# A weight's last rows on few partitions: 32 partitions in two steps instead of 20 in three, read as eight groups of four rows instead of five

## The chip, the cores and the metric

The kernel runs on one core of one Trainium2 chip. The metric is the device time of one execution, in microseconds (us), as the median of several runs; lower is better. The profile comes from one further execution that was recorded instruction by instruction and packet by packet.

## The reference, cut to what matters

One decoding step for a batch of two sequences: a layer norm, grouped-query attention over a cache of 4096 positions (16 query heads, 8 key and value heads, head size 256), and a bilinear gated unit whose result gates the attention's output.

```python
x = A_x                                     # (2, 1, 448)
xn = _layernorm(x, axis=-1)
s = _A_ref(xn, A_k_cache, A_v_cache, A_wq, A_wo)
g = _silu(_B_ref(xn, B_w_gate, B_w_up, B_w_down))
return x + s * g

# _A_ref
q = (x @ wq).reshape(B, Sq, Hq, Dh).transpose(0, 2, 1, 3)
k = jnp.repeat(k_cache, rep, axis=1)        # 2 query heads share a key head
v = jnp.repeat(v_cache, rep, axis=1)
p = softmax(einsum("bhqd,bhkd->bhqk", q, k) * Dh ** -0.5)
return (einsum("bhqk,bhkd->bhqd", p, v) ...).reshape(B, Sq, Hq * Dh) @ wo

# _B_ref
return ((x @ w_gate) * (x @ w_up)) @ w_down
```

All arrays are float32. The two caches hold 67 MB each; wq (448 x 4096), wo (4096 x 448) and the three matrices of the gated unit (448 x 1792, twice, and 1792 x 448) make up the rest of the 158.6 MB that are read.

## The kernel before

**Loads.** The 16 pairs of a key head and a batch row are worked off one after another; pair i needs `k{i}` (4 MB) and `v{i}` (4 MB). All loads go through one queue, that of the sync engine (SP), in an order fixed by `plan` (lines 85 to 96): `wq0`, `wqx`, `k0`, then the fused loads `vk` (value block i and key block i + 1 in one load of 8 MB), between them the weights (`wgu` after the first, `wdq` after the third, `wo` after the ninth), at the end `k15` and `v14`, and `v15` with the last eight blocks of `wo` in seven pieces. `issue` (line 65) sends the next ones: three at the start, then one or two after the scores of each pair. The tiles of the ring have two buffers and the weights share one slot, so that a load waits until the buffer's last reader is done. The 16 DMA engines each take a share of the rows of a load, one after another in the order of the queue.

**The query projection.** `query(0)` makes the queries of the first four key heads from `wq0` and `wqx`, `query(1)` (after pair 4) those of the others from `wq1`, which comes with `wdq`. A weight with 448 rows is folded onto 128 partitions (`folded`, line 444): rows 0 to 383 are three full steps of 128 rows for each of four column tiles (12 blocks of 512 columns), and the last 64 rows of the four tiles, two tiles to a block, are blocks 12 and 13. `rows` (line 191) multiplies: 12 matmuls with the full steps (line 199), then the rest by `last` (line 200), where `xf` holds the normalized input's last 64 values twice, on partitions 0 to 63 and 64 to 127, with zeros beside them, so that one matmul serves two column tiles.

**wqx.** For `wq0` alone, block 12 (the last 64 rows of tiles 0 and 1) isn't loaded on 128 partitions. It comes as `wqx`, on 20 partitions (`SIDE`): three steps (`NS`) of 20 rows for each of the two tiles, and four rows (`LEFT`) of both tiles together on eight partitions; seven pieces of 512 columns in all (`EXTRA`). In main memory it is stored as five groups of four rows with a fifth, empty row behind each (line 456), and the load takes `wqx[:, :4]`. So `wq0` has 13 blocks of 512 columns on 128 partitions. The matmuls are those of lines 206 to 212: six with 20 rows against `xeT`, `last(1, 12)` for block 13 among them, and one with eight rows against `xl`. `xeT` and `xl` are made at the start: transposes at lines 155 and 156, copies at 157 and 161, and two selects on GpSimd (lines 162 to 165) that zero the half of `xl` that belongs to the other tile. Because block 12's second half begins with the four rows that share a piece, `folded` rolls these rows by `LEFT`, and lines 129 and 130 write the normalized input's tail in the same rolled order.

**The rest.** Per pair: scores (line 265), softmax, transposition, values (line 309); the results are collected in `ob` and projected with `wo`. At the end the values of pair 15 (line 409) run as the pieces of `v15` land, and the last blocks of `wo` (lines 413 to 420) as theirs land. `manual_schedule` keeps the order of the code on each engine.

Of the kernel before, what the change touches and what calls it, by code (L numbers as in the profile page):

```python
# [10 lines left out]
OP = mybir.AluOpType  # L11
AX = mybir.AxisListType

B, D = 2, 448
HKV, REP, SK, DH = 8, 2, 4096, 256
F = 1792
NT = 4
W = 32
DUP = W // 2
NK = 4  # L20
# [6 lines left out]
LATE = 24  # L27
THIRD = [24, 25, 26, 28, 29, 30, 31, 27]
PART = 14 * (D + 512)
SIDE = 20  # L30
NS = 3
EXTRA = 2 * NS + 1
LEFT = 64 - NS * SIDE
EPS = 1e-5


# [5 lines left out]
def gated_decode_block(ctx: ExitStack, tc: tile.TileContext, x, first, vk, last0, last1, wq0, wqx, wdq, wo, wgu, out):  # L42
    nc = tc.nc
# [11 lines left out]
    def bank(name=None):  # L55
        return psum.tile([128, 512], F32, name=name, bufs=1) if name else two()[:, 0]
# [8 lines left out]
    def issue(n=1):  # L65
        for names, src, cuts in todo[:n]:
# [12 lines left out]
            if names == ["wq0"]:  # L79
                at = src.shape[1]  # L80
                loaded["wqx"] = t[:, at:at + EXTRA * 512]
                nc.sync.dma_start(loaded["wqx"][:SIDE], wqx[:, :4])
        del todo[:n]
# [23 lines left out]
    ident = const.tile([128, 128], F32)  # L107
# [6 lines left out]
    xc = e0[:, 1, :D]  # L114
# [8 lines left out]
    rstd = const.tile([B, 1], F32)  # L123
# [2 lines left out]

    xn = e1[:, 1]
    nc.vector.tensor_scalar(xn[:, :D], xc, rstd, None, op0=OP.mult)  # L128
    nc.vector.tensor_scalar(xn[:, D:D + LEFT], xc[:, D - LEFT:], rstd, None, op0=OP.mult)
    nc.vector.tensor_scalar(xn[:, D + LEFT:], xc[:, 384:D - LEFT], rstd, None, op0=OP.mult)  # L130
    pt = bank()
    for k in range(NK):
        nc.tensor.transpose(pt[:, B * k:B * (k + 1)], xn[:, k * 128:(k + 1) * 128], ident[:B, :B])  # L133
    def copies(dst, pt):
        n, b = pt.shape
        nc.vector.tensor_copy(dst.rearrange("p k (b j) -> p k b j", b=B),
                              pt.rearrange("p (k b) -> p k b", b=B)[:, :, :, None].to_broadcast([n, b // B, B, DUP]))
# [5 lines left out]
    spare = oT1.rearrange("p g d r m -> p (g d r) m")  # L143

    xf = spare[:, NK:NK + 2]
# [4 lines left out]

    xeT = spare[:SIDE, :NS]
    pt = bank()
    for j in range(NS):
        at = 384 + j * SIDE
        nc.tensor.transpose(pt[:SIDE, B * j:B * (j + 1)], xn[:, at:at + SIDE], ident[:B, :B])
    nc.tensor.transpose(pt[:2 * LEFT, B * NS:B * (NS + 1)], xn[:, D - LEFT:D + LEFT], ident[:B, :B])
    copies(xeT, pt[:SIDE, :NS * B])

    xl = spare[:2 * LEFT, NK + 2:NK + 4]
    for a in range(2):  # L160
        copies(xl[:, a:a + 1], pt[:2 * LEFT, NS * B:(NS + 1) * B])
    nc.gpsimd.affine_select(out=xl, in_=xl, compare_op=OP.is_ge, fill=0.0, base=0, pattern=[[-LEFT, 2], [0, W]],
                            channel_multiplier=1)
    nc.gpsimd.affine_select(out=xl, in_=xl, compare_op=OP.is_ge, fill=0.0, base=LEFT - 1, pattern=[[LEFT, 2], [0, W]],
                            channel_multiplier=-1)

    both = work.tile([128, D], F32, name="h")[:B, :W].rearrange("p (b j) -> p b j", b=B)
    nc.vector.tensor_copy(both, ident[:B, :B, None].to_broadcast([B, B, DUP]))
    pt = bank()
    for c in range(NT):  # L170
        nc.tensor.matmul(pt[W * c:W * (c + 1), :SL], both.rearrange("p b j -> p (b j)"), x2[:, c * SL:(c + 1) * SL],
                         start=True, stop=True)
# [18 lines left out]
    def rows(ps, w, n, extra=None):  # L191


        def block(i):
            return w[:, i * n:(i + 1) * n]

        for k in range(3):
            for c in range(NT):
                nc.tensor.matmul(ps[W * c:W * (c + 1), :n], xnT[:, k, :], block(NT * k + c), start=k == 0, stop=False)  # L199
        def last(a, i):  # L200
            nc.tensor.matmul(ps[64 * a:64 * (a + 1), :n], xf.rearrange("p a j -> p (a j)"), block(i), start=False, stop=True)  # L201

        if extra is not None:

            for j in range(NS):
                for c in range(2):
                    at = (c * NS + j) * n
                    nc.tensor.matmul(ps[W * c:W * (c + 1), :n], xeT[:, j, :], extra[:SIDE, at:at + n], start=False, stop=False)  # L208
                if j == 0:
                    last(1, 12)  # L210
            nc.tensor.matmul(ps[:2 * W, :n], xl.rearrange("p a j -> p (a j)"), extra[:2 * LEFT, 2 * NS * n:(2 * NS + 1) * n],  # L211
                             start=False, stop=True)
            return
        for a in range(2):
            last(a, 12 + a)


    qT = [const.tile([128, B, 4, 2, REP, DUP], F32, name=f"qT{h}") for h in range(2)]
# [1 line left out]
    def query(h):  # L220
        ps = bank()
        rows(ps, loaded[f"wq{h}"], 512, None if h else loaded["wqx"])
        for r in range(REP):
            nc.vector.transpose(qT[h][:, :, :, :, r, :].rearrange("p b g d j -> p (g d) b j"),
                                ps[:, r * 256:(r + 1) * 256])
# [16 lines left out]
    def ffn_in():  # L242
        pp = two()
        for i, w in enumerate(("wg", "wu")):
            rows(pp[:, i], loaded[w], FC)
        g = work.tile([128, FC], F32, name="h")
        nc.scalar.copy(g, pp[:, 0, :FC])
        h = work.tile([128, FC], F32, name="h")
        nc.vector.tensor_mul(h, pp[:, 1, :FC], g)
        nc.vector.transpose(hT.rearrange("p i m -> p (i m)"), h)  # L250
# [34 lines left out]
    def softmax(i, s, m, pT=None):  # L285
        sm = bank("sm")
        nc.tensor.transpose(sm[:1, :128], m[:, 0:1], ident)  # L287
        mx = work.tile([1, NT, W], F32, name="mx", bufs=1)
        nc.vector.tensor_reduce(  # L289
            mx, sm[:1, None, :128].rearrange("p o (c j) -> p o j c", c=NT).to_broadcast([1, NT, W, NT]),  # L290
            axis=AX.X, op=OP.max)
        nc.tensor.transpose(sm[:, 128:129], mx.rearrange("p c j -> p (c j)"), one)  # L292
        nc.vector.tensor_scalar(m[:, 1:2], sm[:, 128:129], -1.0 / 16, None, op0=OP.mult)  # L293
        p = work.tile([128, 2, 512], F32, name="p", bufs=1)
        nc.scalar.activation(p, s, AF.Exp, bias=m[:, 1:2], scale=1.0 / 16, accum_out=su[:, place(i):place(i) + 1])  # L295
        if pT is None:
            pT = work.tile([128, 2, 512], F32, name="pT", bufs=1)
        nc.vector.transpose(pT.rearrange("p h n -> p (h n)"), p.rearrange("p h n -> p (h n)"))  # L298
        return pT
# [65 lines left out]
    p = softmax(0, *ss)  # L365
    for i in range(LAST):
# [10 lines left out]
        p = softmax(i + 1, *ss)  # L377
# [19 lines left out]
    ps = [p]  # L397
    project(oT1, 4, EARLY, LATE)

    last = slot.tile([128, PART], F32, name="slot", align_bytes=512)  # L400
    p = softmax(LAST + 1, *ss, last[:, :1024].rearrange("p (h n) -> p h n", h=2))
# [78 lines left out]
```

## Time and profile before

| | |
|---|---|
| median of 3 runs | 376.34 us (376.27 to 376.48) |
| span of the profiled execution | 374.6 us |
| bytes read | 158.56 MB |
| mean granted TensorE clock | 0.775 |

The profiled execution's own time is its span, from the first instruction to the last, and what lies around it. On the page, the 40 digits of a row are the busy share of 40 equal slices of the span, in tenths; the DMA row is a mean over 16 DMA engines. A row of instructions or loads gives the line, the engine, the operation, the tile written and the tiles read, and the number of instructions. In a row of a table by windows stand the window, its length, the busy time of TensorE's matmuls and weight loads, VectorE, ScalarE and GpSimd with the number of instructions of each, the granted clock, the share of the DMA engines' time and GB/s. q1 is SP's queue of loads, q8 and q14 are instruction fetches, q10 is the load of x.

### The profile page before, as it was taken

The page shows a single profiled execution, that of the slowest core. Times are in us where ns is not written, and L with a number is a line of the kernel's source. Part 1 is how long each engine was busy: PE and PEld are TensorE (multiplying, and loading weights), DVE is VectorE, ACT ScalarE, POOL GpSimd, SP SyncE. Part 2 cuts the span into 40 slices and gives each one's busy share as a digit, 9 for nine tenths or more (in the row PEclk, how much of TensorE's full clock was granted, in tenths as well). Part 3 has the DMA queues.
Part 4 walks back from the last instruction along what each step waited for, and adds up shares of the span by engine and source line. Part 5 has one row for each costly group of instructions (what it writes and reads, how often), then busy time and mean ns, then how long its engine had stood idle before and what let it go on. Part 6 is the DMA issues. An engine that isn't in the chain of part 4 may idle for free.

```text
span 374.6 us, 3092 instructions
## 1 busy us (share of the span) xinstructions
PE 197.4 (53%) x1388; PEld 55.3 (15%) x1388; DVE 72.6 (19%) x125; ACT 25.8 (7%) x40; POOL 1.7 (0%) x9
## 2 busy tenths in 40 slices
PE   0793459081726090858271756712718180909785
PEld 0210112020201020212020211200202020202122
DVE  2303030104040003040404050400211212030530
ACT  1001010001020002010101010100010101010121
POOL 0000000000000000000000000000000000000000
PEclk9968596778696587796778696885868586777999
DMA  8999899999999999999999999999999999999994
GB/s 327 435 493 434 376 438 441 448 443 437 431 428 443 441 434 420 422 427 434 436 448 448 427 426 397 452 448 448 436 427 420 436 427 420 448 411 441 411 416 186
DMA packets 4217, 158.81 MB, mean 424 GB/s; under 512 B 599, under 2 KB 857, under 8 KB 1241
## 3 DMA queue, kind: packets, MB, share of 16 engines
q1 hardware_dynamic: 4201, 158.62, 98.2%
q8 instruction: 11, 0.18, 0.2%
q10 hardware_dynamic: 4, 0.00, 0.0%
q14 instruction: 1, 0.01, 0.0%
HBM read 158.56 MB, written 0.06 MB: 423 GB/s over the span
## 4 chain that ended last, share of the span: by engine, by line
DMA 74%; PE 23%; issue 1%; DVE 1%; ACT 0%; POOL 0%; ACTq 0%; SPq 0%; DVEq 0%
DMA ring<-vk 67%; PE o L313 10%; PE s L274 8%; DMA ring<-last 5%; DMA p<-x 2%; PE s L199 1%; PE s L208 1%; PE s L313 1%; PE s L211 1%; PE s L356 0%; PE s L201 0%; PE wide L351 0%; ACT ob L410 0%; PE cb L322 0%; DVE pT L121 0%
## 5 line engine op out<-in xcount | busy, mean ns | idle before, releaser
L313 PE MATMUL o<-ring,pT 128*32 128x512 f32 x480 | 83.2, 856 | 115.6 <-DMA ring<-vk 115.6
L275 DVE TENSOR_REDUCE m<-s 128x1 f32<-128x1024 f32 x16 | 19.6, 1222 | 219.9 <-PE s L274 219.9
L274 PE MATMUL s<-ring,qT 128*32 128x512 f32 x512 | 59.6, 607 | 0.9 <-PE s L211 0.9
L313 PEld LDWEIGHTS o<-ring,pT 128*32 128x32 f32 x480 | 20.8, 150 | 168.6 <-issue 156.1
L295 ACT ACTIVATE p<-s,m 128x1024 f32<-128x1024 f32 x16 | 17.8, 1113 | 286.1 <-DVE m L293 286.1
L274 PEld LDWEIGHTS s<-ring,qT 128*32 128x32 f32 x512 | 17.2, 112 | 40.7 <-issue 38.1
L298 DVE STREAM_TRANSPOSE pT<-p 128x1024 f32<-128x1024 f32 x15 | 18.7, 1245 | 21.2 <-ACT p L295 21.2
L199 PE MATMUL s<-slot,xnT 128*32 128x512 f32 (+1 forms) x96 | 15.3, 788 | 3.3 <-DMA slot<-wgu 3.3
L287 PE MATMUL sm<-ident,m 128*1 128x128 f32 x16 | 4.3, 270 | 18.8 <-DVE m L275 18.8
L289 DVE TENSOR_REDUCE mx<-sm 1x128 f32<-1x512 f32 x16 | 10.7, 671 | 2.9 <-PE sm L287 2.9
L292 PE MATMUL sm<-one,mx 1*128 1x1 f32 x16 | 3.6, 226 | 14.2 <-DVE mx L289 14.2
L373 DVE COPY ob<-o 128x512 f32<-128x512 f32 x14 | 9.5, 681 | 0.0
L256 PE MATMUL s<-slot,hT 128*32 128x448 f32 x28 | 5.8, 918 | 4.4 <-DMA slot<-wdq 4.4
L351 PE MATMUL wide<-slot,oT 128*32 128x448 f32 x48 | 6.4, 684 | 0.7 <-DVE oT L340 0.6
L287 PEld LDWEIGHTS sm<-ident,m 128*1 128x1 f32 x16 | 1.3, 79 | 32.9 <-DVE m L275 32.3
L133 PE MATMUL s<-ident,pT 2*128 2x2 f32 x4 | 0.6, 246 | 10.4 <-DVE pT L128 10.4
L322 PE MATMUL cb<-ob,add_blocks 128*32 128x512 f32 (+2 forms) x48 | 4.1, 456 | 2.4 <-DVE ob L373 1.6
L199 PEld LDWEIGHTS s<-slot,xnT 128*32 128x32 f32 x96 | 3.5, 137 | 11.7 <-issue 11.7
L292 PEld LDWEIGHTS sm<-one,mx 1*128 1x128 f32 x16 | 2.3, 142 | 17.2 <-DVE mx L289 17.2
L295 ACT ACT_TABLE_LOAD x2 | 2.6, 1283 | 30.6 <-DVE m L293 23.5
L313 PE MATMUL s<-ring,slot 128*32 128x512 f32 x32 | 4.2, 600 | 0.8 <-DMA ring<-last 0.8
L201 PE MATMUL s<-slot,oT 128*64 128x448 f32 (+1 forms) x14 | 4.6, 664 | 0.0
(76 smaller groups left out, 47.5 us busy)
## 6 DMA issues: line engine op xcount, KB each, us to landing
ring<-last SPq DMA_DIRECT2D x2, 4096.0 KB, 24.8
slot<-wdq SPq DMA_DIRECT2D x1, 6720.0 KB, 45.5
slot<-wgu SPq DMA_DIRECT2D x1, 6272.0 KB, 32.7
slot<-wo SPq DMA_DIRECT2D x1, 5376.0 KB
ring<-first SPq DMA_DIRECT2D x1, 4096.0 KB, 20.6
slot<-wq SPq DMA_DIRECT2D x1, 3328.0 KB, 10.7
ring<-last SPq DMA_DIRECT2D x1, 2048.0 KB
ring<-last SPq DMA_DIRECT2D x1, 1536.0 KB, 17.8
```

The costliest lines, as they stand in the source:

```text
L199: nc.tensor.matmul(ps[W * c:W * (c + 1), :n], xnT[:, k, :], block(NT * k + c), start=k == 0, stop=False)
L256: nc.tensor.matmul(ps[W * t:W * (t + 1), :D], hT[:, i], loaded["wd"][:, i * D:(i + 1) * D], start=i < NT, stop=i >= 14 - NT)
L274: nc.tensor.matmul(s[W * c:W * (c + 1), h, :], q[:, d], k[:, h, d, c, :], start=d == 0, stop=d == 1)
L275: nc.vector.tensor_reduce(m[:, 0:1], s, axis=AX.XY, op=OP.max)
L287: nc.tensor.transpose(sm[:1, :128], m[:, 0:1], ident)
L289: nc.vector.tensor_reduce(mx, sm[:1, None, :128].rearrange("p o (c j) -> p o j c", c=NT).to_broadcast([1, NT, W, NT]), axis=AX.X, op=OP.max)
L292: nc.tensor.transpose(sm[:, 128:129], mx.rearrange("p c j -> p (c j)"), one)
L295: nc.scalar.activation(p, s, AF.Exp, bias=m[:, 1:2], scale=1.0 / 16, accum_out=su[:, place(i):place(i) + 1])
L298: nc.vector.transpose(pT.rearrange("p h n -> p (h n)"), p.rearrange("p h n -> p (h n)"))
L313: nc.tensor.matmul(o[W * t:W * (t + 1), :], pT[:, h, at:at + 2 * W:2], loaded[f"v{i}"][:, e * 512:(e + 1) * 512], start=e < NT, stop=e >= ...
L351: nc.tensor.matmul(wide[W * t:W * (t + 1), :D], heads(oT, i, first), w, start=i < NT, stop=i >= SIDES - NT)
L373: nc.vector.tensor_copy(ob[:, place(i) % 8], o)
```

## The change

`wqx` now holds the last 64 rows of all four column tiles. It lies on 32 partitions and is used in two steps of 32 rows, eight pieces of 512 columns. In main memory it is stored as eight groups of four rows, again with an empty row behind each. `wq0` keeps the 12 full blocks and loses block 13. The rows no longer need rolling, so the rolled copy of the input, `xl`, its transpose, its copies and its two selects go. The query's matmuls after the 12 full steps are eight with 32 rows, one for each step and tile.

```diff
-SIDE = 20
-NS = 3
-EXTRA = 2 * NS + 1
-LEFT = 64 - NS * SIDE
+SIDE = 32
+NS = 64 // SIDE
+EXTRA = NT * NS
...
-    nc.vector.tensor_scalar(xn[:, D:D + LEFT], xc[:, D - LEFT:], rstd, None, op0=OP.mult)
-    nc.vector.tensor_scalar(xn[:, D + LEFT:], xc[:, 384:D - LEFT], rstd, None, op0=OP.mult)
+    nc.vector.tensor_scalar(xn[:, D:], xc[:, 384:], rstd, None, op0=OP.mult)
...
-    nc.tensor.transpose(pt[:2 * LEFT, B * NS:B * (NS + 1)], xn[:, D - LEFT:D + LEFT], ident[:B, :B])
     copies(xeT, pt[:SIDE, :NS * B])
-
-    xl = spare[:2 * LEFT, NK + 2:NK + 4]
-    for a in range(2):
-        copies(xl[:, a:a + 1], pt[:2 * LEFT, NS * B:(NS + 1) * B])
-    nc.gpsimd.affine_select(out=xl, in_=xl, ...)
-    nc.gpsimd.affine_select(out=xl, in_=xl, ...)
...
         if extra is not None:
-
             for j in range(NS):
-                for c in range(2):
+                for c in range(NT):
                     at = (c * NS + j) * n
-                    nc.tensor.matmul(ps[W * c:W * (c + 1), :n], xeT[:, j, :], extra[:SIDE, at:at + n], start=False, stop=False)
-                if j == 0:
-                    last(1, 12)
-            nc.tensor.matmul(ps[:2 * W, :n], xl.rearrange("p a j -> p (a j)"), extra[:2 * LEFT, 2 * NS * n:(2 * NS + 1) * n],
-                             start=False, stop=True)
+                    nc.tensor.matmul(ps[W * c:W * (c + 1), :n], xeT[:, j, :], extra[:SIDE, at:at + n], start=False, stop=j == NS - 1)
             return
...
-        last = np.concatenate([last[0], np.roll(last[1], LEFT, 0)])
+        last = np.concatenate([last[0], last[1]])
...
     wqx = np.zeros((SIDE // 4, 5, EXTRA * 512), np.float32)
-    t0, t1 = wq0[:64, 12 * 512:13 * 512], wq0[64:, 12 * 512:13 * 512]
-    ends = np.zeros((SIDE, EXTRA, 512), np.float32)
-    ends[:, :NS] = t0[:NS * SIDE].reshape(NS, SIDE, 512).transpose(1, 0, 2)
-    ends[:, NS:2 * NS] = t1[LEFT:].reshape(NS, SIDE, 512).transpose(1, 0, 2)
-    ends[:2 * LEFT, 2 * NS] = np.concatenate([t0[NS * SIDE:], t1[:LEFT]])
+    ends = wq[384:, 0].reshape(NS, SIDE, NT, 512).transpose(1, 2, 0, 3)
     wqx[:, :4] = ends.reshape(SIDE // 4, 4, EXTRA * 512)
-    wq0 = np.concatenate([wq0[:, :12 * 512], wq0[:, 13 * 512:]], 1)
+    wq0 = c(wq0[:, :12 * 512])
```

The load of `wq0` goes from 128 rows of 6656 floats to 128 rows of 6144, that of `wqx` from 20 rows of 3584 floats to 32 rows of 4096. No other load changes, and their order is the same.

More of the change, by code (lines that the diff above doesn't have):

```diff
@@ L155, in gated_decode_block @@
         nc.tensor.transpose(pt[:SIDE, B * j:B * (j + 1)], xn[:, at:at + SIDE], ident[:B, :B])
-    nc.tensor.transpose(pt[:2 * LEFT, B * NS:B * (NS + 1)], xn[:, D - LEFT:D + LEFT], ident[:B, :B])
     copies(xeT, pt[:SIDE, :NS * B])
-    xl = spare[:2 * LEFT, NK + 2:NK + 4]
-    for a in range(2):
-        copies(xl[:, a:a + 1], pt[:2 * LEFT, NS * B:(NS + 1) * B])
[L162 to L165, printed above, removed]
     both = work.tile([128, D], F32, name="h")[:B, :W].rearrange("p (b j) -> p b j", b=B)
@@ L199, in rows @@
                 nc.tensor.matmul(ps[W * c:W * (c + 1), :n], xnT[:, k, :], block(NT * k + c), start=k == 0, stop=False)
-        def last(a, i):
-            nc.tensor.matmul(ps[64 * a:64 * (a + 1), :n], xf.rearrange("p a j -> p (a j)"), block(i), start=False, stop=True)
         if extra is not None:
             for j in range(NS):
-                for c in range(2):
+                for c in range(NT):
                     at = (c * NS + j) * n
-                    nc.tensor.matmul(ps[W * c:W * (c + 1), :n], xeT[:, j, :], extra[:SIDE, at:at + n], start=False, stop=False)
-                if j == 0:
-                    last(1, 12)
-            nc.tensor.matmul(ps[:2 * W, :n], xl.rearrange("p a j -> p (a j)"), extra[:2 * LEFT, 2 * NS * n:(2 * NS + 1) * n],
-                             start=False, stop=True)
+                    nc.tensor.matmul(ps[W * c:W * (c + 1), :n], xeT[:, j, :], extra[:SIDE, at:at + n], start=False, stop=j == NS - 1)
             return
         for a in range(2):
-            last(a, 12 + a)
+            nc.tensor.matmul(ps[64 * a:64 * (a + 1), :n], xf.rearrange("p a j -> p (a j)"), block(12 + a), start=False, stop=True)
     qT = [const.tile([128, B, 4, 2, REP, DUP], F32, name=f"qT{h}") for h in range(2)]
```

## The prediction

> **What bounds the kernel now.** I read the page first: engine totals, the 40 slices, the queues, the chain that ended last.
>
> ```profile
> span 374.6 us, 3092 instructions
> PE 197.4 (53%) x1388; PEld 55.3 (15%) x1388; DVE 72.6 (19%) x125; ACT 25.8 (7%) x40; POOL 1.7 (0%) x9
> DMA  8999899999999999999999999999999999999994
> q1 hardware_dynamic: 4201, 158.62, 98.2%
> q8 instruction: 11, 0.18, 0.2%
> DMA 74%; PE 23%; issue 1%; DVE 1%; ACT 0%; POOL 0%; ACTq 0%; SPq 0%; DVEq 0%
> ```
>
> No compute engine is busy more than 53%; q1, SP's queue of loads, fills 16 DMA engines for 98.2% of the span, from the first slice to the last but one. So I treat the kernel as 16 queues worked off in parallel: a byte more on one engine delays that engine to the end, and the end belongs to the engine that finishes last. The profiled execution took 374.6 us of span; the median of the timed runs is 376.34, so 1.74 us lie around the span and I carry them unchanged.
>
> Speed of one engine, from the queue view of the stretch 30 to 345 us:
>
> ```profile
> q1 hardware_dynamic: 2509, 135.79, 99.6%
> ```
>
> 135.79 MB in 0.996 x 16 x 315 = 5020 engine-us is 27.05 KB (thousands of bytes) per us and engine.
>
> **How far apart the engines are.** Each engine ends its part of a transfer with a write of 4 bytes, and the queue view counts these as "under 512 B". Windows around the end of one transfer therefore count engines. For k0, the windows 19.9 to 21 and 22 to 22.6 us:
>
> ```profile
> DMA packets 27, 0.88 MB, mean 804 GB/s; under 512 B 11, under 2 KB 11, under 8 KB 11
> DMA packets 14, 0.59 MB, mean 983 GB/s; under 512 B 5, under 2 KB 5, under 8 KB 5
> ```
>
> Eleven engines finish k0 about 2 us before five others. The two loads issued before k0 are these:
>
> ```profile
> slot<-wq SPq DMA_DIRECT2D x1, 3328.0 KB, 10.7
> slot<-wqx SPq DMA_DIRECT2D x1, 280.0 KB
> ```
>
> wq0 gives every engine 3328/16 = 208 KiB. wqx, read as five groups of four rows, is the work of five engines, one group each: 56 KiB = 57.3 KB, 57.3/27.05 = 2.12 us, which is the step between eleven and five. I call those "the five".
>
> Next the instruction fetches. Windows 47 to 48.5, then 53.9 to 55.2 and 55.9 to 56.8 us, where wgu ends:
>
> ```profile
> q8 instruction: 1, 0.02, 3.9%
> DMA packets 26, 0.96 MB, mean 736 GB/s; under 512 B 10, under 2 KB 10, under 8 KB 10
> DMA packets 18, 0.79 MB, mean 874 GB/s; under 512 B 6, under 2 KB 6, under 8 KB 6
> ```
>
> One fetch held one engine for 0.039 x 16 x 1.5 = 0.94 us, and one of the eleven now stands beside the five. Following each engine's packets (the next starts within 10 ns of the end of the last), I find the ten such fetches up to 356 us on eight engines in turn, none of the five, the first two of the eight being hit twice. Three engines, outside the five, are never hit. The same count near the end, v14, windows 353.2 to 354.2, 354.2 to 355.2, 355.2 to 356, 356 to 357:
>
> ```profile
> DMA packets 18, 0.41 MB, mean 410 GB/s; under 512 B 3, under 2 KB 3, under 8 KB 3
> DMA packets 22, 0.36 MB, mean 360 GB/s; under 512 B 6, under 2 KB 6, under 8 KB 6
> DMA packets 22, 0.29 MB, mean 369 GB/s; under 512 B 5, under 2 KB 5, under 8 KB 5
> q8 instruction: 1, 0.02, 7.3%
> DMA packets 30, 0.46 MB, mean 459 GB/s; under 512 B 2, under 2 KB 2, under 8 KB 2
> ```
>
> Three engines are a good microsecond ahead of the next and up to 3 us ahead of the last. Six are in the middle; the fetch in the third window (0.073 x 16 x 0.8 = 0.93 us) then hits one of them. The last two are one of the five and an engine that was hit twice. How the last row drains:
>
> ```profile
> 369.00:369.50 0.50, 0.50 (x17) 0.18 (x6) 0.20 (x1) 0.00 (x0) 0.00 (x0) 1.00 0.59 226
> 369.50:370.00 0.50, 0.48 (x6) 0.00 (x0) 0.12 (x1) 0.00 (x0) 0.00 (x0) 1.00 0.31 118
> 370.00:370.50 0.50, 0.41 (x17) 0.44 (x21) 0.00 (x0) 0.46 (x1) 0.00 (x0) 1.00 0.14 54
> 370.50:371.00 0.50, 0.50 (x31) 0.50 (x23) 0.00 (x0) 0.07 (x1) 0.00 (x0) 1.00 0.03 11
> ```
>
> The share next to last, times 16, is the mean number of engines still at work: 9, 5, 2, and in the last half microsecond 0.03 x 16 x 0.5 = 0.24 us of a single one, to about 370.75. By the packets, the twice-hit pair ends at 370.75 and 370.35, the five between 369.7 and 370.3, the three at 367.6 to 367.9, the other six at 369.0 to 369.65.
>
> **Does the end follow the last engine?** The chain of waits in order of time, and two lines of the timeline:
>
> ```profile
> 347.69 17.79 DMA ring<-last
> 365.52 2.30 PE s L313 x16
> 371.07 0.47 PE s L356 x16
> ...
> 365.52 2.28 PE L313 MATMUL s<-ring,slot 128*32 128x512 f32 x16 [0.79 <-DMA ring<-last]
> 366.75 0.15 PEld L313 LDWEIGHTS s<-ring,slot 128*32 128x32 f32 x4 [0.22 <-DMA ring<-last]
> ```
>
> TensorE waits for two pieces of v15 (idle 0.79 and 0.22 us) and then runs the tail without a gap of note. If all pieces land earlier by up to 0.79 us, the tail moves with them; beyond that the matmuls before L313 hold it.
>
> **The change part by part.**
>
> *wq0 loses a block.* 13 x 512 floats a row become 12 x 512. Each engine has eight rows: 8 x 2048 = 16.4 KB less, 16.4/27.05 = -0.61 us on all 16.
>
> *wqx grows.* Eight groups of four rows of 8 x 512 floats: 4 x 16384 = 65.5 KB, 2.42 us, on eight engines. The five pay 2.42 - 2.12 - 0.61 = -0.30 us. Three further engines pay 2.42 - 0.61 = +1.82 us (unrounded). The remaining eight gain 0.61 us. In the Trainium skill, "DMA: Bandwidth & Descriptors", section on why a DMA increments its semaphore by 16, a load runs on the largest number up to 16 that divides both sides' slowest dimensions, from the lowest-numbered engines up; the five 4-byte writes of k0's late group agree with the five groups here, and by it the change uses engines 0 to 7.
>
> *Which three?* If they are the three idle ones, the ends become: twice-hit pair 370.75 - 0.61 = 370.14 and 369.74, the five at most 370.00, the three 367.9 + 1.82 = 369.7, the six 369.05 at most. The last engine moves by -0.61. I take this: the fetches go round eight engines that exclude the five, five and three make the other eight, and a ring over one half of 16 is the plain reading. No row names an engine, so the other end stays as a rival. The same page (section "Latency and other measured facts") says that engines 7 and 15 are usually slower; by it engine 7 would be a poor place for 64 KiB more. If it were a late engine, the price would be the first rival's; the page itself suspects loads issued from GpSimd, and these come from SP; no run here shows an engine by number.
>
> *Compute that goes or changes* (start of the timeline, and a row of the loads issued):
>
> ```profile
> 11.34 0.84 DVE L136 COPY oT<-s 64x32 f32<-64x32 f32 x5
> 12.56 0.23 POOL L164 TENSOR_SCALAR_AFFINE_SELECT oT<-oT 8x64 f32<-8x64 f32 x1
> 18.18 1.12 PE L208 MATMUL s<-slot,oT 20*32 20x512 f32 x4
> 22.29 1.96 PE L211 MATMUL s<-slot,oT 8*64 8x512 f32 x2
> 24.29 0.34 SPq L78 DMA_DIRECT2D slot<-wgu  x1
> slot<-wgu SPq DMA_DIRECT2D x1, 6272.0 KB, 32.7
> ```
>
> Two transposes, two of five copies, one small scaling (L129) and both selects on GpSimd go. Of the query's matmuls after the twelve full ones, 16 passes (6.07 us, from 18.18 to 24.25) become 16 passes of the L208 kind: 16 x 1.12/4 = 4.5 us. So query(0) ends some 1.5 us earlier, or, at L211's 0.98 us a pass, 9.6 us later. Neither counts: the wgu load that waits for it is issued at 24.29 and lands at 57.0, while its own bytes take 6272 KiB/16/27.05 = 14.8 us; so it starts to move at 42 us, behind k0 and vk0 in the queue, 17 us after its issue. That load is the cover; without it each microsecond would be one. I cost this edit at nothing, as I do the 24 KiB less in all (0.06 us spread over 16 engines, already in the terms).
>
> *Code.* Two transposes less are four TensorE instructions of 2776; the 11 fetches come about every 252, so each comes some 0.5 us later. The one at 355.4 still comes before the end; nothing moves to another engine.
>
> *Unknown: how the engines start.* They finish wq0 spread over 0.85 us:
>
> ```profile
> DMA packets 36, 0.49 MB, mean 490 GB/s; under 512 B 16, under 2 KB 16, under 8 KB 16
> ```
>
> (window 10.2 to 11.2 us, all 16 writes). The one that ends last began some 0.4 us late. If that does not repeat, the five at 370.00 set the end: -0.75. If one of the five draws it instead, 370.4: -0.35. I take -0.55, a little less than the sum, for other draws can only add a late engine.
>
> Sum on the profile: 374.6 - 0.55 = 374.05; with 1.74 around it **375.8 us**, own range 375.4 to 376.2.
>
> **The rivals.**
>
> *Slower: the three further engines are among those that fetch.* Then an engine with one or two fetches also gets 64 KiB more and decides the end. Three neighbours among eight: with the last one in it 370.75 + 1.82 = 372.57, so +1.82, 378.2 us; with the second but not the last 370.35 + 1.82, +1.4, 377.7; otherwise at best 369.65 + 1.82 = 371.45, +0.7, 377.0. It decides as soon as one fetching engine that ends later than 370.75 - 1.82 = 368.93 takes a group, and all eight do. For it: no row tells engines by number. Against: the split of 5 + 3 and 8. 0.30.
>
> *Hidden: the tail turns out bound by compute.* The transpose, projection and sum after L313 run back to back, so a gain in loads might stop there: 376.2 to 376.4. Against: the two waits on loads that end at 365.52 and 366.75. 0.06.
>
> *The read does not go to eight engines.* On all 16, each engine would get 1.21 - 0.61 = +0.61: the last at 371.36, 377.0; on four, 4.85 - 0.61 = +4.2 on engines that lose 2.12: about +1.6, 378. Against: five groups made five engines. 0.06.
>
> **How the numbers follow.** Forecast 0.58, rivals 0.30, 0.06, 0.06. 0.2% is 0.75 us, about what a measurement of this kernel can tell from no change: 375.59 to 377.09. The forecast lies inside with 0.47 and below with 0.11, since its best case is -0.75 to -0.79. The first rival puts 0.09 inside (377.0) and 0.21 above; the second is inside; the third, the likelier of whose cases is four, I count above. Faster 0.11, same 0.62, slower 0.27. Range 375.4 to 377.8: it leaves out 0.04 below and the 378 cases, 0.15, above.
>
> **What would show it.** The wqx load of 512 KB; at the end of k0 eight late engines instead of five, still about 2.4 us behind; at the end of v14 no group of three 2 us ahead of the rest; the last half microsecond with a single engine in it gone; L313's wait for loads shorter by 0.6 us at most. Wrong would be: an engine that ends v14 after 357.5 us, one with both a group of wqx and a fetch of 0.9 us, or three engines still early.

## The result: 0.15% slower, and a profile after in which one engine ends last by itself

| | before | after |
|---|---|---|
| median | 376.24 us (376.00 to 376.90, 22 runs) | 376.56 us (376.34 to 378.03, 22 runs) |
| runs above 377.3 us | 0 of 22 | 5 of 22 |
| span of the profiled execution | 374.6 us | 375.9 us |

The ratio is 1.0015, with a 95% interval of 1.0009 to 1.0021. The changed kernel is slower, not 0.5 us faster as forecast, though the difference is within 0.2%. Its runs fall into two groups: 17 from 376.34 to 376.98 us and five from 377.57 to 378.03 us. Below these are called the lower and the upper group (some of the texts on record say "slow group" for the upper one). The granted TensorE clock does not tell them apart: 0.760 to 0.782 in the five, 0.749 to 0.780 in the others. The profiled execution, 377.8 us, is one of the five, so its span shows the upper group and not the median.

The page of the changed kernel:

```profile
span 375.9 us, 3081 instructions
PE 190.5 (51%) x1386; PEld 54.6 (15%) x1386; DVE 72.3 (19%) x122; ACT 25.8 (7%) x40; POOL 1.3 (0%) x7
DMA  8999999899999999999999999999999999999993
q1 hardware_dynamic: 4216, 158.59, 97.8%
q8 instruction: 11, 0.18, 0.2%
```

The bound is as before: q1 fills the 16 DMA engines for 97.8% of the span, and 11 instruction fetches (q8) come. The two loads that the change touches, and the queue view of k0's end, windows 19.3 to 20.5 and 21.6 to 22.4 us:

```profile
slot<-wq SPq DMA_DIRECT2D x1, 3072.0 KB, 10.3
slot<-wqx SPq DMA_DIRECT2D x1, 512.0 KB
DMA packets 24, 0.79 MB, mean 655 GB/s; under 512 B 8, under 2 KB 8, under 8 KB 8
DMA packets 22, 0.92 MB, mean 1147 GB/s; under 512 B 8, under 2 KB 8, under 8 KB 8
```

Eight engines end k0 early and eight late, where there were 11 and 5: eight groups are read by eight engines. Now the end of v14, windows 352.7 to 355, 355 to 355.6, 355.9 to 357, 357.7 to 358.2 us:

```profile
DMA packets 47, 1.03 MB, mean 449 GB/s; under 512 B 7, under 2 KB 7, under 8 KB 7
DMA packets 18, 0.21 MB, mean 355 GB/s; under 512 B 5, under 2 KB 5, under 8 KB 5
q8 instruction: 1, 0.02, 9.2%
DMA packets 32, 0.49 MB, mean 447 GB/s; under 512 B 3, under 2 KB 3, under 8 KB 3
DMA packets 15, 0.21 MB, mean 418 GB/s; under 512 B 2, under 2 KB 2, under 8 KB 2
```

Seven engines are through v14 first, then five, then three. In the last window one of the two small packets is the end of v14; the other is an early engine's end of the next piece. So one engine ends v14 at 357.93 us, 1.1 us after any other. It is the one that the fetch of the second window (355.30 us) held: the packet behind that fetch is the one that ends at 357.93 us. Before, the last one was at 356.61. The drain of the last row, in the table by windows:

```profile
370.00:370.50 0.50, 0.46 (x17) 0.47 (x20) 0.00 (x0) 0.00 (x0) 0.00 (x0) 1.00 0.18 68
370.50:371.00 0.50, 0.50 (x14) 0.12 (x5) 0.25 (x1) 0.00 (x0) 0.00 (x0) 1.00 0.12 47
371.00:371.50 0.50, 0.47 (x10) 0.07 (x7) 0.06 (x1) 0.02 (x1) 0.00 (x0) 1.00 0.06 25
```

From 371.0 on the share of 0.06 x 16 is a single engine. The tail waits for it, as the timeline and the chain of waits show:

```profile
366.99 2.26 PE L294 MATMUL s<-ring,slot 128*32 128x512 f32 x16 [1.65 <-DMA ring<-last]
368.19 0.14 PEld L294 LDWEIGHTS s<-ring,slot 128*32 128x32 f32 x4 [0.20 <-DMA ring<-last]
...
347.57 19.37 DMA ring<-last
366.99 2.29 PE s L294 x16
```

The matmuls of v15 (L294, L313 before) start at 366.99 instead of 365.52 us. That is 1.47 us, and it is 1.3 us at the end of the span: 375.9 against 374.6.

Which engine is it? It has wqx and two instruction fetches, that of 355.30 us and an earlier one. The end of vk2 shows the earlier one alone, windows 92 to 94.3, 94.3 to 95.6 and 95.6 to 97 us, first of the kernel before:

```profile
DMA packets 24, 0.88 MB, mean 381 GB/s; under 512 B 9, under 2 KB 9, under 8 KB 9
DMA packets 22, 0.81 MB, mean 620 GB/s; under 512 B 7, under 2 KB 7, under 8 KB 7
DMA packets 10, 0.54 MB, mean 384 GB/s; under 512 B 0, under 2 KB 0, under 8 KB 0
```

and of the changed kernel, with the fetch in the window 80 to 81.5 us ahead of them:

```profile
q8 instruction: 1, 0.02, 3.7%
DMA packets 28, 1.17 MB, mean 508 GB/s; under 512 B 8, under 2 KB 8, under 8 KB 8
DMA packets 17, 0.54 MB, mean 414 GB/s; under 512 B 7, under 2 KB 7, under 8 KB 7
DMA packets 16, 0.81 MB, mean 576 GB/s; under 512 B 1, under 2 KB 1, under 8 KB 1
```

Two fetches have come by this time, at 46.8 and 80.2 us. An engine outside wqx with one of them ends at 94.3 us, near the engines with wqx. Only an engine with both can end vk2 in the third window. Before there is none; after there is one, at 96.10 us by its packets, against 94.5 to 95.0 for seven others with wqx. So engines that fetch are among the three that the change adds.

### The profile page after: what moved, and what is told of

It is laid out like the page before. It is cut to its first block, busy times and chain, and to the rows that moved or that the text cites. A ratio compares the mean times of both kernels' runs of the same rounds, so it can differ in the third digit from the quotient of the medians.

```text
span 375.9 us, 3081 instructions
## 1 busy us (share of the span) xinstructions
PE 190.5 (51%) x1386; PEld 54.6 (15%) x1386; DVE 72.3 (19%) x122; ACT 25.8 (7%) x40; POOL 1.3 (0%) x7
## 3 DMA queue, kind: packets, MB, share of 16 engines
q1 hardware_dynamic: 4216, 158.59, 97.8%
## 4 chain that ended last, share of the span: by engine, by line
DMA 78%; PE 20%; issue 0%; SPq 0%; ACT 0%; DVE 0%
DMA ring<-vk 67%; PE o L294 10%; PE s L255 8%; DMA ring<-first 5%; DMA ring<-last 5%; PE s L294 1%; PE s L337 0%; SPq L81 0%; PE wide L332 0%; ACT ob L391 0%; PE cb L303 0%; SPq L77 0%; PE sm L287 0%; DVE gate L403 0%; DVE gate L404 0%
## 5 line engine op out<-in xcount | busy, mean ns | idle before, releaser
L294 PE MATMUL o<-ring,pT 128*32 128x512 f32 x480 | 81.3, 839 | 120.0 <-DMA ring<-vk 120.0
L255 PE MATMUL s<-ring,qT 128*32 128x512 f32 x512 | 60.7, 616 | 2.7 <-DMA ring<-first 2.7
L294 PEld LDWEIGHTS o<-ring,pT 128*32 128x32 f32 x480 | 20.6, 148 | 171.3 <-issue 158.1
L255 PEld LDWEIGHTS s<-ring,qT 128*32 128x32 f32 x512 | 17.7, 114 | 42.2 <-issue 42.2
L332 PE MATMUL wide<-slot,oT 128*32 128x448 f32 x48 | 4.9, 543 | 1.2 <-DMA slot<-wo 0.6
L294 PE MATMUL s<-ring,slot 128*32 128x512 f32 x32 | 4.2, 599 | 2.4 <-DMA ring<-last 2.4
L276 ACT ACT_TABLE_LOAD x2 | 2.6, 1283 | 32.8 <-DVE m L274 25.4
L274 DVE TENSOR_SCALAR m<-sm 128x1 f32<-128x1 f32 x16 | 2.5, 158 | 5.1 <-PE sm L273 5.1
## 6 DMA issues: line engine op xcount, KB each, us to landing
ring<-first SPq DMA_DIRECT2D x1, 4096.0 KB, 20.5
```

The lines of the kernel that those rows point to most:

```text
L255: nc.tensor.matmul(s[W * c:W * (c + 1), h, :], q[:, d], k[:, h, d, c, :], start=d == 0, stop=d == 1)
L294: nc.tensor.matmul(o[W * t:W * (t + 1), :], pT[:, h, at:at + 2 * W:2], loaded[f"v{i}"][:, e * 512:(e + 1) * 512], start=e < NT, stop=e >= ...
L332: nc.tensor.matmul(wide[W * t:W * (t + 1), :D], heads(oT, i, first), w, start=i < NT, stop=i >= SIDES - NT)
```

## The experiments

The engines are counted here by the groups of wqx that they carry: the sixth, seventh and eighth are the three that the change adds. No row names an engine, and the "upper eight" are the ones that carry no group when there are eight. (Some of the texts on record count from 0, so that their engines 5, 6 and 7 are these three.)

Theory A: two of the three added engines fetch instructions, and where the round of fetches begins differs from execution to execution. Theory B: the fetching eight are the upper eight, as predicted, and the loss is elsewhere. Theory C: the compute of the new form costs the time.

**Numbering the engines** (`probe_before`, `probe_after`): 15 small loads behind the first vk.

```diff
     issue(3)
+
+    mark = const.tile([15, 15 * 3], F32)
+    for n in range(1, 16):
+        nc.sync.dma_start(mark[:n, (n - 1) * 3:n * 3], first[:n, :3])
```

> The kernel before, with 15 loads of 1, 2, ... 15 rows of 12 bytes added behind the first vk load, into a tile that nobody reads: the engine that comes n-th in a load's order takes a row of 16 - n of them, so the count of 12-byte packets numbers the engines. Theory A (the eight engines that fetch instructions are a fixed set of neighbours, of which two are numbers 6 and 7 or 5 and 6, so that two of the three engines that the change adds to wqx fetch as well; which of the eight fetches first differs from execution to execution): the fetching eight are 6 to 13 or so, not 8 to 15; the engines of wqx are 0 to 4. Theory B (the eight are numbers 8 to 15, as predicted, and the change is slower for another reason): the fetching eight are 8 to 15 and 5, 6, 7 have none. Span 374.6 to 375.2 us in both.

> The changed kernel with the same 15 loads. Theory A: wqx on engines 0 to 7, and two of these have instruction fetches; an engine that carries wqx and one fetch ends last at some 371.0 us, with two fetches at some 372.1 us, so the span is 374.7 or 375.9 us, by where the round of fetches began in this execution. Theory B: no fetch on 0 to 7.

They took 384.3 and 383.5 us, one run each, with spans of 382.4 and 381.7 us, some 6 to 8 us more than expected: the 120 small packets stall the queues between 39 and 46 us, and the engines come out of it in an order that I could not follow packet by packet. So the engines stay without numbers, and the probes decide nothing between A and B. They give a third and a fourth list of fetches, whose durations come in the same cyclic order as in the others.

**Sixteen groups** (`groups16`): each engine gets two rows of wqx.

```diff
-nc.sync.dma_start(loaded["wqx"][:SIDE], wqx[:, :4])
+nc.sync.dma_start(loaded["wqx"][:SIDE], wqx[:, :2])
-    wqx = np.zeros((SIDE // 4, 5, EXTRA * 512), np.float32)
+    wqx = np.zeros((SIDE // 2, 3, EXTRA * 512), np.float32)
-    wqx[:, :4] = ends.reshape(SIDE // 4, 4, EXTRA * 512)
+    wqx[:, :2] = ends.reshape(SIDE // 2, 2, EXTRA * 512)
```

> The changed kernel, wqx stored and read as sixteen groups of two rows instead of eight of four; compute as in the changed kernel. Every engine then pays 8 packets of 2 KB less in wq0 (-0.61 us) and two rows of 16 KB (+1.21 us). Theory A: the last engine is one that fetches twice, without wqx's 2.42 us: 0.6 us later than in the kernel before, 376.8 to 376.9 us (ratio 1.0016), and no run above 377.3 us, against 5 of 22 runs at 377.6 to 378.0 of the changed kernel. Theory C (the shortened wq0 or the query's new matmuls cost the time, not the engines): as the changed kernel, with the same group of runs above 377.5 us.

Measured: 378.59 us (378.01 to 379.80, 6 runs; before 376.20 beside them), ratio 1.0053 with an interval of 1.0039 to 1.0067. Theory A's range is missed by 1.7 us, and theory C, which expected the changed kernel's times, misses too. A new cost hides the answer: the 16 KB packets of wqx took 1.25 us in the middle of the load, where they take 0.61 us in the changed kernel, and the first 32 KB packets of k0 behind them took up to 2.6 us instead of 1.21.

**The seventh and eighth engine freed** (`six`): the last eight rows go as two loads of four rows, one row to an engine, meant for the first four engines.

```diff
-nc.sync.dma_start(loaded["wqx"][:SIDE], wqx[:, :4])
+nc.sync.dma_start(loaded["wqx"][:24], wqx[:6, :4])
+nc.sync.dma_start(loaded["wqx"][24:28], wqx[6, :4])
+nc.sync.dma_start(loaded["wqx"][28:32], wqx[7, :4])
```

> The changed kernel, but rows 24 to 31 of wqx are read as two loads of four rows each, one row an engine on engines 0 to 3, so that engines 6 and 7 carry nothing of wqx and engines 0 to 3 carry 6 rows instead of 4 (3.63 us). Theory A: no engine carries both wqx and a 16 KB fetch; 0 to 3 end at 367.1 + 3.6 = 370.7 us, or 371.5 us where the one 8 KB fetch of the trace hits one of them; the engines that fetch twice end at 370.0 to 370.3 us: 376.4 to 377.2 us, and no run above 377.4 us. If engine 5 is one that fetches, the group of slow runs stays. Theory C: the slow group stays as well, since the compute is that of the changed kernel.

Measured: 380.24 us (380.06 to 380.74, 4 runs), ratio 1.0103 with an interval of 1.0089 to 1.0116. Missed again, by the same cost and more of it: the packets of the two added loads took up to 2.4 us each, and in the same stretch k0's packets of 32 KB on the other engines took up to 4.06 us instead of 1.21. The window 12 to 17 us, first of the changed kernel, then of this one:

```profile
DMA packets 75, 2.20 MB, mean 439 GB/s; under 512 B 8, under 2 KB 8, under 8 KB 8
DMA packets 49, 1.03 MB, mean 206 GB/s; under 512 B 13, under 2 KB 13, under 8 KB 13
```

While rows 24 to 31 are read, all 16 engines together move less than half of what they move in the changed kernel. So these two say nothing about A against C, and the next kernels keep four rows of neighbouring partitions on one engine, as both given kernels do.

**Six, seven, eight engines, and five** (`half6`, `half7`, `half8`, `half5`): wq0 as before the change (13 blocks), wqx holds block 12 alone, in steps of 24, 28, 32 or 20 rows. The compute goes without the leftover piece, the rolled rows and the selects, as in the changed kernel, but block 13 stays with wq0. Among the four, the number of engines that carry wqx differs, and with it what each of them carries: 65.5 KB on five engines, 49.2 KB on six and on seven, 32.8 KB on eight. The edit of `half6`, against the kernel before:

```diff
-SIDE = 20
-NS = 3
-EXTRA = 2 * NS + 1
-LEFT = 64 - NS * SIDE
+SIDE = 24
+NS = 3
+EXTRA = 2 * NS
...
                 for c in range(2):
                     at = (c * NS + j) * n
-                    nc.tensor.matmul(..., extra[:SIDE, at:at + n], start=False, stop=False)
-                if j == 0:
-                    last(1, 12)
-            nc.tensor.matmul(ps[:2 * W, :n], xl..., extra[:2 * LEFT, ...], start=False, stop=True)
+                    nc.tensor.matmul(..., extra[:SIDE, at:at + n], start=False, stop=j == NS - 1)
+            last(1, 12)
...
+    ends = np.zeros((NS * SIDE, 2, 512), np.float32)
+    ends[:64] = np.stack([wq0[:64, 12 * 512:13 * 512], wq0[64:, 12 * 512:13 * 512]], 1)
+    ends = ends.reshape(NS, SIDE, 2, 512).transpose(1, 2, 0, 3)
```

> The kernel before (wq0 keeps 13 blocks, wqx holds block 12 alone), with wqx on 24 partitions, read as six groups of four rows of 6 x 512 floats (49 KB, 1.82 us an engine, 8 rows of it padding) in three steps of 24 rows; no leftover piece and no selects. Nothing changes for the engines outside the first six. Theory A (the eight engines that fetch instructions include the last two of the first eight, but not the sixth; which of the eight begins the round differs between executions; an engine with wqx and a fetch ends last): as the kernel before, 376.0 to 376.9 us, ratio within 0.9990 to 1.0010, and no engine with wqx has a 16 KB fetch. Theory B (the fetching eight are the upper eight): the same time here. If the sixth engine fetches, runs with 369.5 + 1.4 = 370.9 us for it, or 372.3 us where it fetches twice, show up as runs above 377.3 us.

> As the kernel half6 with seven groups of four rows (28 partitions, 6 x 512 floats a row, the same 1.82 us an engine). Theory A: the seventh engine fetches, so that it ends at 369.5 + 1.4 = 370.9 us in executions where it fetches once and at 372.3 us where it fetches twice (two of the eight places where the round can begin): 376.5 us in most runs and some at 377.8 to 378.1 us. Theory B: no change against half6.

> As half6 with eight groups of four rows (32 partitions, two steps, 4 x 512 floats a row, 32.8 KB, 1.21 us an engine). Theory A: the seventh and eighth engine fetch; they end at 367.7 + 1.21 + 1.41 = 370.3 us with one fetch and at 371.7 us with two (three of eight places): 376.0 to 376.5 us in most runs, and a group at 377.2 to 377.5 us, 0.5 us below the slow group of the changed kernel. Theory B: 0.3 us faster than before, since the five end earlier.

> As half6 with five groups of four rows (20 partitions, four steps, 8 x 512 floats a row, 65.5 KB, 2.42 us an engine, of which a fifth is padding): the compute of the changed kernel's kind, without leftover piece, rolled rows or selects, and the loads on the five engines of the kernel before, 0.30 us more on each. Theory A (the sixth and the seventh engine fetch instructions, the first five don't, so a piece on six, seven or eight engines meets fetches and a piece on five does not): the five end at 370.0 us, 370.6 us for the one with the 8 KB fetch, no later than the engines that fetch twice (370.3 to 370.9 us): 376.1 to 376.5 us in most runs, none above 377.3 us, ratio 0.9995 to 1.0010. Theory C (the compute of the new form costs the time): as the changed kernel, ratio 1.0015 to 1.0026, with runs above 377.5 us.

The changed kernel ran once more beside the first three (`after_again`):

> The changed kernel once more, for another profile. Theory A: two groups of runs, at 376.3 to 377.0 and at 377.5 to 378.1 us. In a profile of the lower group the two engines that carry wqx and fetch do so once each; the packets of the ten fetches before 370 us come in the same cyclic order as in the other profiles, from another start. Theory B or any other reason outside the engines: the round begins at the same engine in every profile, and the two groups differ in something else (clock, start of the loads).

| kernel | engines with wqx | median, us | runs above 377.3 us | ratio, 95% interval |
|---|---|---|---|---|
| half5 | 5 | 376.58 | 0 of 11 | 1.0007 (0.9998 to 1.0016) |
| half6 | 6 | 376.63 | 4 of 11, up to 378.06 | 1.0017 (1.0006 to 1.0029) |
| half7 | 7 | 376.85 | 5 of 12, up to 378.02 | 1.0019 (1.0008 to 1.0029) |
| half8 | 8 | 376.79 | 3 of 12, up to 377.40 | 1.0012 (1.0003 to 1.0020) |
| after_again | 8 | 376.96 | 4 of 9, up to 378.20 | 1.0026 (1.0014 to 1.0037) |

The kernel before had none above 377.3 us in the 33 runs beside half6 to after_again (up to 377.02) nor in the 15 beside half5 (up to 376.88).

*half6* has an upper group already, so the sixth engine fetches: theory A is right in kind, but I had put its two engines one place too high. Its profile shows the meeting at the end of vk12, windows 314.5 to 316, 316 to 317.5 and 317.6 to 319 us:

```profile
DMA packets 8, 0.33 MB, mean 218 GB/s; under 512 B 3, under 2 KB 3, under 8 KB 3
DMA packets 27, 0.98 MB, mean 655 GB/s; under 512 B 12, under 2 KB 12, under 8 KB 12
DMA packets 9, 0.52 MB, mean 374 GB/s; under 512 B 1, under 2 KB 1, under 8 KB 1
```

Three engines have neither load nor fetch, twelve have one of the two, one has both and comes last, at 317.96 us. Following its packets, it stood 0.86 us for the fetch at 263.4 us, and the packet behind the fetch took 2.97 us instead of 2.42: 1.41 us for one fetch.

*half7* has two such engines. One of them was hit twice in the profiled execution (378.02 us); the end of vk2, windows 94.3 to 95.6 and 95.6 to 97 us, has the same lone engine as the changed kernel:

```profile
DMA packets 21, 0.75 MB, mean 579 GB/s; under 512 B 7, under 2 KB 7, under 8 KB 7
DMA packets 13, 0.65 MB, mean 461 GB/s; under 512 B 1, under 2 KB 1, under 8 KB 1
```

*half8* adds no third. The end of vk12, windows 314.5 to 315.5, 315.5 to 317.1 and 317.2 to 319 us, after one fetch on each of the eight engines:

```profile
DMA packets 7, 0.33 MB, mean 328 GB/s; under 512 B 2, under 2 KB 2, under 8 KB 2
DMA packets 24, 0.79 MB, mean 492 GB/s; under 512 B 12, under 2 KB 12, under 8 KB 12
DMA packets 15, 0.85 MB, mean 473 GB/s; under 512 B 2, under 2 KB 2, under 8 KB 2
```

Two engines have neither load nor fetch, twelve have one of the two, two have both. So of the first eight engines the sixth and seventh fetch, and the eighth does not; the other six fetching engines are among the upper eight, and theory B falls. The upper group of half8, 377.38 to 377.40 us, lies where its smaller load puts it (expected 377.2 to 377.5). Its other runs do not all lie where they were expected: four of the twelve are at 376.0 to 376.5 us, five at 376.7 to 377.1. Why was not looked into.

*half5* has no engine with both, and no upper group: none of 11 runs, where the changed kernel had 9 of 31 (at that share none in 11 would come up by chance some 2% of the time). Its profiled execution, 376.23 us, begins the round of fetches where the first profiled execution of the changed kernel does: the same engine of the round fetches twice, at 81 and 355 us, and ends at 370.3 us, against 372.1 us with wqx on top. (It carries no wqx here; it is told by its stalls of 0.86 to 0.87 us, which only the sixth and seventh engine show in the profiles above, the others 0.90 to 0.95.) Window 95.6 to 97 us:

```profile
DMA packets 8, 0.43 MB, mean 307 GB/s; under 512 B 0, under 2 KB 0, under 8 KB 0
```

Its median, 376.58 us, is a little above the range that I had written (376.1 to 376.5); with an interval of 0.9998 to 1.0016 it can be told neither from the kernel before nor from the changed kernel's 1.0015. So half5 shows what makes the upper group, not what moves the other runs by 0.3 us.

Theory C falls by the changed kernel's own first profile, for half5's query is not that of the changed kernel (two tiles in four steps, with block 13 apart):

```profile
18.13 1.92 PE L193 MATMUL s<-slot,oT 32*32 32x512 f32 x16
20.11 0.33 SPq L77 DMA_DIRECT2D slot<-wgu  x1
22.71 6.35 PE L255 MATMUL s<-ring,qT 128*32 128x512 f32 x32 [2.66 <-DMA ring<-first]
```

The new matmuls are shorter than the old ones, the wgu load behind them is issued 4.2 us earlier (20.11 against 24.29), and the first scores (L255) then wait 2.66 us for k0. At the end TensorE waits for v15, as shown above. The new compute is nowhere late.

*after_again* has two groups as the first time. Its profiled execution, 376.58 us, is of the lower one. The end of v14, windows 355 to 356, 356 to 357 and 357.2 to 358.2 us:

```profile
DMA packets 31, 0.44 MB, mean 442 GB/s; under 512 B 7, under 2 KB 7, under 8 KB 7
DMA packets 27, 0.39 MB, mean 393 GB/s; under 512 B 3, under 2 KB 3, under 8 KB 3
q8 instruction: 1, 0.02, 6.0%
DMA packets 28, 0.43 MB, mean 434 GB/s; under 512 B 1, under 2 KB 1, under 8 KB 1
```

No engine ends v14 after 356.76 us (the one small packet of the last window is an early engine's end of the next piece, at 357.70). The two engines with both ended the last row at 370.92 us, each hit once, at 157 and 196 us; in the first profile they were hit first at 81 and 123 us. So the round began elsewhere, with the same kernel. The five profiled executions of kernels with such engines agree with this as the difference of the two groups: 377.80 and 378.02 us (the changed kernel's first, half7), where one of them is hit twice, 376.29 to 376.58 us (half6, half8, after_again), where none is. The unprofiled runs are sorted by their times alone. What decides where the round begins was not tried.

## Why the prediction was wrong, by its own steps

- **The bound, right.** The span is 16 queues, and the end belongs to the last engine: in the profiles of the kernel before, the changed kernel (two) and half5 to half8 the span ends 3.8 to 3.9 us after the last engine's end, which lies between 370.61 us (half5) and 372.31 us (half7).
- **What the loads cost an engine, right.** The engine that is through first, without load or fetch, ends 0.59 us earlier for the shorter wq0 (367.64 us before, 367.05 after). The group of eight ends k0 2.4 us late. The engines with wqx and no fetch end at 369.3 to 369.5 us (before: 369.7 to 369.9), each time but for one, at 370.3. The engine that fetches at 81 and 355 us ends 1.8 us later with the changed kernel's loads (372.1) than with half5's, where it carries no wqx (370.3). All this is within about 0.1 us of what was worked out.
- **"Which three?" This step failed.** "I take this: the fetches go round eight engines that exclude the five, five and three make the other eight, and a ring over one half of 16 is the plain reading." The eight are not one half. They are the sixth and seventh engine and six of the upper eight, so only one of the three that got a group was idle. The prediction put the three at 367.9 + 1.82 = 369.7 us; two of them ended at 372.1 and 371.0 us in the first profile and both at 370.92 in the second, so the last engine, which was to end 0.61 us before 370.75, ended after it in both. The prediction had the opposite case as its first rival, at 0.30, and gave it the right mechanism.
- **The price of a fetch was read too low, without harm to the sum.** The row of q8 gives 0.94 us for the fetch itself. The packet behind it was stretched by 0.55 us as well: 1.41 us in all. The forecast and its rival took the engines' ends from the packets, with the whole price in them. The group of wqx added 1.82 us, as said, so an engine with one fetch ended at 370.9 us, where the engines that fetched twice had ended at 370.4 and 370.8 us before the change.
- **One profile was taken for the place of the fetches.** I read which engines are hit twice from one execution and kept it. It changes. By the profiles, the lower group (376.34 to 376.98 us) is the case in which neither of the two engines is hit twice, the upper one (377.57 to 378.03, 1.3 to 1.8 us above 376.24) that in which one is; the upper one is near the rival's 377.7 and 378.2 us. The first case holds most of the runs, so the median moved by 0.3 us only. In the profiles of the kernel before and of after_again the last engine ends at 370.77 and at 370.92 us, with spans of 374.6 and 374.8 us, which accounts for part of that 0.3 us; the rest stays open, the more so as half5, with no such engine, has nearly the same median.
- **Compute at nothing, right, with one size off.** The 16 new passes took 1.92 us, not the 4.5 that were worked out from L208, so the query ended some 4 us earlier instead of 1.5. It made no difference, since the scores then wait for k0.

Of what the prediction named as a sign of being wrong, two came: an engine that ends v14 after 357.5 us, and one that carries a group of wqx and a fetch. That the median, 376.56 us, lies within the range of 375.4 to 377.8 us is no merit of the path that was taken: the range holds part of the rival's times.

No version here beats the kernel before. Its five engines are the ones that never showed a 16 KB fetch, and the next engine in line is one that does.

## What to carry to other kernels

When all DMA engines are busy from start to end, count bytes and interruptions for each engine, not the mean; a balance that looks free in one profile may lean on engines that something else also uses. Count small end-of-transfer packets in windows to see the engines apart, and do it in two profiles: what differs between executions is not yours to plan with. Where no row tells which engine is which, add the load to one engine more at a time; the first that meets the fetches shows as a second group of runs (four of 11 in half6, 1.5 us above its other runs), more plainly than in the median (0.4 us).

## What the hardware showed unasked

- The instruction fetches go round eight of the 16 engines in one cyclic order, in all profiles of this study in which I could follow it, and begin at different engines in different executions of the same kernel.
- A load whose rows put two engines on the same four neighbouring partitions ran at half speed an engine (groups16: 1.25 us for 16 KB against 0.61), and with four engines on four partitions at a quarter to a third (six: 2.0 to 2.4 us in the later packets). That the shared partitions are the reason is argued from these two layouts; it was not varied by itself. It is not the whole of it: engines that were already at k0, on other partitions too, slowed down in the same stretch (32 KB in up to 4.06 us instead of 1.21 in six, up to 2.6 in groups16).
- Fifteen loads of 12-byte rows, 120 packets, cost some 6 to 8 us of span (probe_before 382.4 us against 374.6, probe_after 381.7 us against 374.8 and 375.9).
